# Scores from one product over 192 keys in two runs, in an attention and MoE kernel whose order is drawn by a planner

## The chip, the core and the metric

One core of a Trainium2 chip runs the kernel. The metric is the device time of one execution in microseconds (us). The profile is of one execution. The engines are TensorE (PE; its weight loads are PEld), VectorE (DVE), ScalarE (ACT), GpSimd (POOL) and SyncE (SP), which issues the DMAs.

## What is computed

An attention with a local window and a few global keys, and behind it a gated mixing layer (the code calls it MoE). Batch 4, 8 heads of 64 dimensions, 768 positions.

```python
scores = scale * np.matmul(q, k.transpose(0, 1, 3, 2))
is_global = pos[None, :] < int(n_global)          # 8
is_local = (rel >= 0) & (rel < int(n_local))      # 96
dist = np.where(is_global & ~is_local, float(n_local), np.abs(rel).astype(np.float32))
scores = scores + (-slopes[:, None, None] * dist[None, :, :])[None]
scores = np.where(is_global | is_local, scores, -1000000000.0)
a = np.exp(scores - np.max(scores, axis=-1, keepdims=True))
a = a / (np.sum(a, axis=-1, keepdims=True) + 1e-09)
x = np.matmul(a, v)                               # then heads side by side: 512 columns
...
h = gelu(x @ w_in); u, v = halves of h
v_s = np.einsum('ts,bsd->btd', w_sg, layernorm(v) * g_ln) + b_sg
out = x + (u * v_s) @ w_out
```

## The kernel before

*Attention units.* The attention is cut into 48 units `n`: a batch, a pair of heads `j`, and a third `u` of the sequence, which holds two tiles `i` of 128 queries. A half of a tile is 64 queries (`e`, `HQ`). Since the window is at most 97 wide (`NL_FAST`) and at most 32 first keys are global (`NG`), 64 queries need 192 keys (`W`): 96 near ones which both halves of the tile share, 64 others of the half's own, and the 32 first keys of the sequence. The first tile of a sequence (`u == 0 and i == 0`) needs just its own 128 keys.

*Tiles.* `load_qk` (L773) brings one tile `qk` per unit: 256 columns of queries, then up to 448 of keys (`KW`), laid out on the host by `unit_keys`. Three such tiles exist. `load_v` brings `v` in the key order that the p.v products want. The array of TensorE is used in quarters of 64x64: `h` (the head) picks the rows, `e` the output partitions, so four products run side by side. MoE products use the whole array.

*A unit's steps.* `score` (L786) fills two PSUM banks `s_ps`, one a head. `softmax` (L813) adds the bias row and takes the minimum of the negated scores on VectorE (L825), does exp with its sum on ScalarE (L830), then the reciprocal (L843). The first 16 units (`TURNS`) turn the probabilities with products against a diagonal (`turn_quarters`, `tps`, L929) and copy them to `pt` on ScalarE or VectorE (L937, L938). The later units scale them on GpSimd or another engine (L851), transpose blocks on VectorE (`tt`, L893) and send them through DRAM and back (`far`, L901 and L905) into `pt`. `weigh` (L941) then multiplies with `v`: a first part, and a second part `again` that follows after a score group has gone between. From unit 20 on two units go together.

*Bias.* `dist` is made once, at the start, on VectorE (L734 to L745) from tiles that GpSimd's iota fills; `build_bias` (L763) multiplies it by a head's slope into `bias[:, h]`. The two heads of a pair keep their 192 keys in two orders (the 96 shared keys and the 32 first ones in the first 128 columns for one head, in the last 128 for the other), so that a row is 2 x 192 + 128 = 512 wide. The last 128 are for the first tile of a sequence.

*MoE.* Each output tile is a row of products in threes (L466 to L468: high by high, high by low, low by high), 128x384 or 128x512. `v_tile`, `u_tile`, `mix_tile` and `out_tile` give these; their results go through ScalarE and VectorE.

*The order.* Nothing is issued in the order in which it is written. `Plan` collects operations with prices by engine, draws 40 sets of rules and shifts from a fixed seed (`search`, L253), orders the work by each (`order`, L278), and keeps the one that ends first by its own prices. It knows that going from whole-array to quarter products and back costs time (`TO_QUARTERS`, `FROM_QUARTERS`, L103), prices a score group at 0.56 or 0.67 (L811), a load by its width (`wire`, L770), and holds `dist` back to a fixed time (`dist_b.since`, L753). Within the first 29 us `keep_on` (L404) fills expected idle time of TensorE with products of zeros (L415). The instructions of each engine then run in the order found. So any changed price or time can move work on every engine.

Of the kernel before, what the change touches and what calls it, by code (L numbers as in the profile page):

```python
# [19 lines left out]
P = 128  # L20
# [8 lines left out]
NG = 32  # L29
# [7 lines left out]
W = P + HQ  # L37
KW = 3 * P + HQ
VT = 2 * P
# [34 lines left out]
def unit_widths(u):  # L74

    return (P + NG + P + NG, P + VT) if u == 0 else (KW, 2 * VT)


def unit_keys(u):

    t, first = 2 * u * P, list(range(NG))
    if u == 0:
        return list(range(P)) + first + list(range(P - NG, 2 * P))
    return (list(range(t - 3 * NG, t - NG)) + first + list(range(t - NG, t + P)) + first
            + list(range(t + P - NG, t + 2 * P)))
# [563 lines left out]
def local_global_attention_moe(tc, qk_in, v_in, q_t, k_t, v_n, n_gl, w_in, g_ln, w_sg_t, b_sg,  # L649
# [43 lines left out]

    bias = cp.tile([P, H, 2 * W + P], BF16, name="bias")

# [4 lines left out]
    rel, key, tmp = (zp.tile([P, W + P], BF16, tag=f"gt{i}", name="setup") for i in (1, 2, 3))  # L700
    dist = zp.tile([P, 2 * W + P], BF16, tag="gt0", name="dist")
    for p0, shared, other in ((0, NG, 3 * NG), (HQ, 3 * NG, 0)):
        ps = slice(p0, p0 + HQ)
        iota(rel[ps, 0:NG], S, 0, 0)
        iota(rel[ps, NG:P], shared, -1, 1)
        iota(rel[ps, P:W], other, -1, 1)
    iota(key[:, 0:NG], 0, 1, 0)
    iota(key[:, NG:W], S, 0, 0)
    iota(rel[:, W:W + P], 0, -1, 1)
# [23 lines left out]
    def distances():  # L733
# [7 lines left out]
        vec.scalar_tensor_tensor(tmp, rel, nl, key, ALU.is_ge, ALU.mult)  # L741
        vec.scalar_tensor_tensor(dist[:, 0:W], rel[:, 0:W], nl, tmp[:, 0:W], ALU.min, ALU.max)
        vec.scalar_tensor_tensor(dist[:, 2 * W:], rel[:, W:], nl, tmp[:, W:], ALU.min, ALU.max)
        for src, dst, n in ((0, HQ, P), (P, 0, HQ)):
            vec.tensor_copy(dist[:, W + dst:W + dst + n], dist[:, src:src + n])  # L745

# [16 lines left out]
    def build_bias(j):  # L763
        for h in (2 * j, 2 * j + 1):
            op([("DVE_SB", 0.22, 0.3, lambda h=h: nc.vector.tensor_scalar(
                bias[:, h], dist, -(2.0 ** (2 - h)), None, ALU.mult)),
                on_act(2 * W + P) + (lambda h=h: nc.scalar.mul(
                    bias[:, h], dist, -(2.0 ** (2 - h))),)], [dist_b], [(bias_b, h)])
# [17 lines left out]
    def score(n, after):  # L786

        b, j, u = units[n]
        qk = loaded.pop(n)
        s_ps = scores[n] = [bank("s_ps", 2 * W) for _ in range(2)]  # L790

        def part(h, e, i, k0, c0, n):
            rows, qc = slice(h * D, (h + 1) * D), i * P + e * HQ
            nc.tensor.matmul(s_ps[h][e * HQ:(e + 1) * HQ, i * W + c0:i * W + c0 + n],  # L794
                             qk[rows, qc:qc + HQ], qk[rows, QW + k0:QW + k0 + n],
                             start=True, stop=True)

        def put():
            quarters = [(h, e) for h in range(2) for e in range(2)]
            for i in range(2):  # L800
                if u == 0 and i == 0:
                    for h, e in quarters:
                        part(h, e, i, 0, 0, P)
                    continue

                for h, e in quarters:
                    part(h, e, i, window(u, i, e)[0], 0 if h == i else HQ, P)
                for h, e in quarters:
# [69 lines left out]
    def turn_blocks(n):  # L878
# [20 lines left out]
        def there():  # L899
# [8 lines left out]

        order = [0, 1, 2, 4, 3] if own else [0, 2, 1, 3, 5, 4]
        turned[n] = to, lambda rows, a, q0, q1: to[  # L910
            rows, q0 // QB:q1 // QB, order[a] * QB:(order[a] + 1) * QB]

    def turn_quarters(n):

        own, ps, diag = units[n][2] == 0, soft.pop(n), diags.pop(n)
        at = [(0, c) for c in ((0, W) if own else (0, 2 * P, P))] + [
            (1, c) for c in (0, 2 * P, P)]
        nt = len(at)
# [22 lines left out]
    def weigh(ns):  # L941
# [21 lines left out]
        def shared(m, second):  # L963
            for r, h in quarters:
                i = (r + h + second) % 2

                part(m, i, r, h, v0[i] + h * D, a0[i] + (i + h) % 2, 0, P,
                     start=not second and m == 0)

        def put():  # L970
            for m in range(len(ns)):
                shared(m, 0)
                for e in range(2):
                    for r, h in quarters:
                        i = (r + h) % 2
                        if u or i:
                            part(m, i, r, h, v0[i] + P + e * D, a0[i] + 2, e * HQ, (e + 1) * HQ,
                                 start=False)
# [417 lines left out]
```

## Time and profile before

| what | value |
|---|---|
| timed runs | 420.73, 421.56, 422.47 us; median 421.56 |
| span of the profiled execution | 420.1 us (the page gives no other time for it) |
| mean granted clock of TensorE | 0.993 |
| bytes read and written in HBM | 48.89 MB and 18.35 MB, 160 GB/s over the span |
| TensorE instructions | 5224 products and as many weight loads |

A row of the groups has line, engine, operation, output<-input tiles, shape and count, then busy time and the mean of one in ns, then the engine's idle time just before such instructions and what ended it. A row of the timeline has start, duration, engine, line, operation, tiles, shape and count. Durations of TensorE's products overlap, so the distance from start to start tells what one costs. The first 85 us hold most of the attention of the first batch, before MoE work is there in plenty; from about 100 us TensorE has MoE products to put between attention steps, and the last 75 us are MoE alone.

### The profile page before, as it was taken

How to read it: one execution, taken by the hardware profiler on the slowest of the kernel's cores; microseconds unless marked ns; L12 is line 12 of the kernel's file. 1: busy time of each engine (PE TensorE's matmuls, PEld its weight loads, DVE VectorE, ACT ScalarE, POOL GpSimd, SP SyncE). 2: the span in 40 equal slices, each digit the busy share in tenths (PEclk: the TensorE clock that was granted, in tenths of full speed). 3: DMA queues.
4: the chain of work that ended last, by engine and by line, in shares of the span. 5: the costliest groups of instructions: out<-in, count | busy, mean ns of one | idle time of the engine just before them, and what ended most of it. 6: DMA issues, size and time to landing. Idle time of an engine off the chain costs nothing.

```text
span 420.1 us, 13632 instructions
## 1 busy us (share of the span) xinstructions
PE 403.7 (96%) x5224; PEld 368.2 (88%) x5224; DVE 323.5 (77%) x1037; ACT 228.2 (54%) x744; POOL 174.6 (42%) x306
## 2 busy tenths in 40 slices
PE   8888989999999999999999999999999999999994
PEld 5766867899998889799999989999999888999994
DVE  6787989999997699995777899885768578754362
ACT  5898889765765765753356556653255343311220
POOL 2234447365686646353554355442553122303100
PEclk9999999989999999999999999999999999999998
DMA  7666575526877778754798785562886521001002
GB/s 246 201 208 166 154 238 153 158 81 173 240 249 255 192 228 238 208 162 114 211 271 227 226 240 141 155 170 54 244 281 172 152 85 39 2 2 48 29 0 81
DMA packets 50040, 68.20 MB, mean 162 GB/s; under 512 B 5809, under 2 KB 33969, under 8 KB 49969
## 3 DMA queue, kind: packets, MB, share of 16 engines
q1 hardware_dynamic: 49968, 67.26, 54.7%
q8 instruction: 43, 0.70, 0.8%
q14 instruction: 29, 0.23, 0.2%
HBM read 48.89 MB, written 18.35 MB: 160 GB/s over the span
## 4 chain that ended last, share of the span: by engine, by line
PE 79%; ACT 6%; DVE 5%; DMA 4%; issue 3%; POOL 1%; SPq 1%; DVEq 0%; POOLq 0%; ACTq 0%
PE mm_ps L466 22%; PE mm_ps L467 21%; PE mm_ps L468 21%; PE s_ps L794 6%; PE av L959 6%; PE tps L929 2%; ACT p L830 2%; DMA pt<-far 2%; DMA qk<-in_qk_in_dram 1%; DMA far<-tt 1%; DVE p L825 1%; DMA v<-in_v_in_dram 1%; ACT stage L631 1%; ACT wsg L641 1%; ACT pt L937 0%
## 5 line engine op out<-in xcount | busy, mean ns | idle before, releaser
L830 ACT ACTIVATE p<-p,pst 128x192 f32<-128x192 f32 (+1 forms) x192 | 84.0, 440 | 36.8 <-DVE pst L825 34.9
L466 PE MATMUL mm_ps<-wsg,z 128*128 128x384 f32 x192 | 65.5, 341 | 0.1
L467 PE MATMUL mm_ps<-wsg,z 128*128 128x384 f32 x192 | 64.9, 338 | 0.0
L468 PE MATMUL mm_ps<-wsg,z 128*128 128x384 f32 x192 | 64.8, 338 | 0.0
L825 DVE CUSTOM_DVE_ANT_0 p<-s_ps,bias 128x192 f32<-128x192 f32 (+1 forms) x192 | 56.5, 337 | 5.1 <-PE s_ps L794 4.9
L851 POOL TENSOR_SCALAR p<-p,pst 128x192 f32<-128x192 f32 (+1 forms) x111 | 50.4, 470 | 15.0 <-DVE pst L843 14.8
L959 PE MATMUL av<-pt,v 64*64 64x128 f32 (+1 forms) x1408 | 47.6, 250 | 1.2 <-DMA pt<-far 1.2
L592 POOL TENSOR_TENSOR o<-o,x 128x384 f32<-128x384 f32 x28 | 28.4, 1013 | 47.5 <-DVE o L589 25.8
L794 PE MATMUL s_ps<-qk 64*64 64x128 f32 (+1 forms) x1408 | 43.1, 249 | 4.1 <-issue 2.5
L794 PEld LDWEIGHTS s_ps<-qk 64*64 64x64 f32 x1408 | 37.1, 134 | 8.9 <-issue 5.7
L466 PE MATMUL mm_ps<-x,win 128*128 128x384 f32 x128 | 44.0, 343 | 0.7 <-ACT pt L937 0.7
L959 PEld LDWEIGHTS av<-pt,v 64*64 64x64 f32 x1408 | 37.2, 134 | 8.2 <-issue 4.9
L468 PE MATMUL mm_ps<-gt,wout 128*128 128x384 f32 x128 | 43.1, 336 | 0.1
L466 PE MATMUL mm_ps<-gt,wout 128*128 128x384 f32 x128 | 43.1, 337 | 0.0
L467 PE MATMUL mm_ps<-gt,wout 128*128 128x384 f32 x128 | 42.9, 335 | 0.0
L468 PE MATMUL mm_ps<-x,win 128*128 128x384 f32 x128 | 42.9, 335 | 0.0
L467 PE MATMUL mm_ps<-x,win 128*128 128x384 f32 x128 | 42.9, 335 | 0.0
L466 PE MATMUL mm_ps<-win,x 128*128 128x512 f32 x96 | 39.6, 412 | 0.0
L500 ACT CAST gt<-y 128x384 fp32r<-128x384 f32 x27 | 13.8, 511 | 46.2 <-DVE y L561 33.4
L467 PE MATMUL mm_ps<-win,x 128*128 128x512 f32 x96 | 37.7, 393 | 0.0
L468 PE MATMUL mm_ps<-win,x 128*128 128x512 f32 x96 | 37.6, 392 | 0.0
L466 PEld LDWEIGHTS mm_ps<-wsg,z 128*128 128x128 f32 x192 | 36.5, 190 | 1.1 <-issue 0.5
(109 smaller groups left out, 905.2 us busy)
## 6 DMA issues: line engine op xcount, KB each, us to landing
qk<-in_qk_in_dram SPq DMA_DIRECT2D x32, 352.0 KB, 3.9
far<-tt SPq DMA_DIRECT2D x96, 96.0 KB, 2.6
pt<-far SPq DMA_DIRECT2D x24, 384.0 KB, 3.9
v<-in_v_in_dram SPq DMA_DIRECT2D x32, 256.0 KB, 3.7
out_dram<-o SPq DMA_DIRECT2D x32, 192.0 KB, 2.7
qk<-in_qk_in_dram SPq DMA_DIRECT2D x16, 288.0 KB, 3.8
v<-in_v_in_dram SPq DMA_DIRECT2D x16, 192.0 KB, 3.6
far<-tt SPq DMA_DIRECT2D x32, 80.0 KB, 2.2
```

The source lines that it names most:

```text
L466: mm(ps.ap, ah, bh, start=(i == 0), stop=False)
L467: mm(ps.ap, ah, bl, start=False, stop=False)
L468: mm(ps.ap, al, bh, start=False, stop=(i == n - 1))
L500: put(out[:, 0, :], src.ap)
L592: lo = lambda eng: eng.tensor_tensor(o.ap, o.ap, xm[:, 1, :].bitcast(F32), ALU.add)
L631: op([on_act(n, 0.07) + (lambda: nc.scalar.mul(f.ap, words()[:, :, 1].bitcast(F32), 2.0 ** -112),)], [raw], [f])
L794: nc.tensor.matmul(s_ps[h][e * HQ:(e + 1) * HQ, i * W + c0:i * W + c0 + n], qk[rows, qc:qc + HQ], qk[rows, QW + k0:QW + k0 + n], start=Tru ...
L825: nc.vector.tensor_tensor_reduce(out=p[:, g, 0:nk], in0=s_ps[h][:, i * W:i * W + nk], in1=bias[:, 2 * j + h, w0:w0 + nk], op0=ALU.add, op1 ...
L830: op([on_act(nk, 0.225) + (lambda p=p, g=g, nk=nk, i=i: nc.scalar.activation(p[:, g, 0:nk], p[:, g, 0:nk], AF.Exp, bias=st[:, 0, i, g:g + ...
L851: op([on_pool_ts(nk, -0.10) + (partial(scaled, lambda o, a, c: nc.gpsimd.tensor_scalar(o, a, c, 1.0, ALU.mult, ALU.mult)),), on_act(nk, 0. ...
L929: nc.tensor.matmul(tps[r][g * HQ:(g + 1) * HQ, a * HQ:(a + 1) * HQ], pc[rows, c:c + HQ], diag[rows, 2 * i + c // W], start=True, stop=True)
L959: nc.tensor.matmul(to, v[rows, vc:vc + D], of, stop=True, skip_group_check=True, **kw)
```

## The change

The host lays the 192 keys of each half-tile out as two runs of 96: `near` (the 96 shared keys), and `before` or `after` (the 32 first keys and the half's own 64). A tile's three runs stand one behind the other, six runs a unit, so that `KW` becomes 576 and `qk` 832 columns wide, keys first and queries behind them. The first keys stand there twice for each tile. A score product then reads both runs with one access pattern (`p (b k)`, step 96 or 192) and writes 192 columns at once; before, it took a product over 128 keys and one over 64. Both heads have the same key order now: the bias row is 192 + 128 = 320 wide, `dist` needs no second copy, `turn_blocks`, `turn_quarters` and `weigh` pick their columns by other indices, and the host swaps the halves of `v` rows for one head. The price of a score in the plan stays; that of a bias row and `dist_b.since` (6.35 to 6.0) fall.

```diff
-KW = 3 * P + HQ
+NS = P - NG
+KW = 6 * NS
...
+def tile_keys(t):
+    first = list(range(NG))
+    return (list(range(t - NG, t + HQ)), first + list(range(t - 3 * NG, t - NG)),
+            first + list(range(t + HQ, t + P)))
...
 def window(u, i, e):
     if u == 0:
-        return P, (NG, 2 * P)[e]
-    return ((HQ, (0, HQ + P)[e]) if i == 0 else (2 * P, (HQ + 3 * NG, 3 * P)[e]))
+        return 0, (NS, NS + P)[e]
+    return 3 * NS * i, 3 * NS * i + NS * (1 + e)
...
-    bias = cp.tile([P, H, 2 * W + P], BF16, name="bias")
+    bias = cp.tile([P, H, W + P], BF16, name="bias")
...
-        vec.scalar_tensor_tensor(dist[:, 0:W], rel[:, 0:W], nl, tmp[:, 0:W], ALU.min, ALU.max)
-        vec.scalar_tensor_tensor(dist[:, 2 * W:], rel[:, W:], nl, tmp[:, W:], ALU.min, ALU.max)
-        for src, dst, n in ((0, HQ, P), (P, 0, HQ)):
-            vec.tensor_copy(dist[:, W + dst:W + dst + n], dist[:, src:src + n])
+        vec.scalar_tensor_tensor(dist, rel, nl, tmp, ALU.min, ALU.max)
...
-    dist_b.since = 6.35
+    dist_b.since = 6.0
...
-            op([("DVE_SB", 0.22, 0.3, lambda h=h: nc.vector.tensor_scalar(
+            op([("DVE_SB", 0.17, 0.25, lambda h=h: nc.vector.tensor_scalar(
                 bias[:, h], dist, -(2.0 ** (2 - h)), None, ALU.mult)),
-                on_act(2 * W + P) + (lambda h=h: nc.scalar.mul(
+                on_act(W + P) + (lambda h=h: nc.scalar.mul(
...
-        def part(h, e, i, k0, c0, n):
-            rows, qc = slice(h * D, (h + 1) * D), i * P + e * HQ
-            nc.tensor.matmul(s_ps[h][e * HQ:(e + 1) * HQ, i * W + c0:i * W + c0 + n],
-                             qk[rows, qc:qc + HQ], qk[rows, QW + k0:QW + k0 + n],
-                             start=True, stop=True)
+        q0 = unit_widths(u)[0]
+        def part(h, e, i):
+            rows, qc = slice(h * D, (h + 1) * D), q0 + i * P + e * HQ
+            to, n = s_ps[h][e * HQ:(e + 1) * HQ], W
+            if u == 0 and i == 0:
+                keys, n = qk[rows, NS:NS + P], P
+            else:
+                near, far = window(u, i, e)
+                step = far - near
+                keys = qk[rows, near:near + 2 * step].rearrange("p (b k) -> p b k", k=step)[:, :, 0:NS]
+                to = to[:, i * W:(i + 1) * W].rearrange("p (b k) -> p b k", k=NS)
+            if n == P:
+                to = to[:, i * W:i * W + n]
+            nc.tensor.matmul(to, qk[rows, qc:qc + HQ], keys, start=True, stop=True)
...
-                for h, e in quarters:
-                    part(h, e, i, window(u, i, e)[0], 0 if h == i else HQ, P)
-                for h, e in quarters:
-                    part(h, e, i, window(u, i, e)[1], P if h == i else 0, HQ)
+                for h in range(2):
+                    for e in range(2):
+                        part(h, e, i)
...
-                w0, nk = (2 * W, P) if own else (g * W, W)
+                w0, nk = (W, P) if own else (0, W)
...
-        order = [0, 1, 2, 4, 3] if own else [0, 2, 1, 3, 5, 4]
         turned[n] = to, lambda rows, a, q0, q1: to[
-            rows, q0 // QB:q1 // QB, order[a] * QB:(order[a] + 1) * QB]
+            rows, q0 // QB:q1 // QB, a * QB:(a + 1) * QB]
...
-                part(m, i, r, h, v0[i] + h * D, a0[i] + (i + h) % 2, 0, P,
+                g = (h - i) % 2
+                a = g if u == 0 and i == 0 else (0, 2 - r)[g]
+                part(m, i, r, h, v0[i] + h * D, a0[i] + a, 0, P,
                      start=not second and m == 0)
```

The order of TensorE's instructions moves with it; lines of the changed kernel are 8 further down (L466 is L474, L794 is L812, L959 is L967). In the rows that follow `s_ps<-qk` is a score product, `av<-pt,v` a p.v product, `tps<-diag,p` a transpose by product, and `mm_ps` a MoE product. The first place is after some 210 us of before, in the steady part; before it stood, on TensorE:

```order
L467 MATMUL mm_ps<-gt,wout 128x384
L468 MATMUL mm_ps<-gt,wout 128x384
L794 MATMUL s_ps<-qk 64x128 x4
L794 MATMUL s_ps<-qk 64x64 x4
L794 MATMUL s_ps<-qk 64x128 x4
L794 MATMUL s_ps<-qk 64x64 x4
L959 MATMUL av<-pt,v 64x128 x4
L959 MATMUL av<-pt,v 64x64 x8
```

In the changed program the same place on TensorE reads:

```order
L476 MATMUL mm_ps<-gt,wout 128x384
L812 MATMUL s_ps<-qk 64x192 x8
L474 MATMUL mm_ps<-x,win 128x384
L475 MATMUL mm_ps<-x,win 128x384
L476 MATMUL mm_ps<-x,win 128x384
L967 MATMUL av<-pt,v 64x128 x4
L967 MATMUL av<-pt,v 64x64 x8
```

Sixteen score products became eight, and three MoE products moved in between the score group and the p.v products.

The second place is the one at about 82 us of before, where unit 15 is turned; TensorE's rows there in before:

```order
L468 MATMUL mm_ps<-wsg,z 128x384
L959 MATMUL av<-pt,v 64x128 x4
L959 MATMUL av<-pt,v 64x64 x4
L929 MATMUL tps<-diag,p 64x64 x20
L794 MATMUL s_ps<-qk 64x128 x4
L794 MATMUL s_ps<-qk 64x64 x4
```

And in the changed program, on TensorE, from the same transposes on:

```order
L967 MATMUL av<-pt,v 64x64 x4
L937 MATMUL tps<-diag,p 64x64 x20
L474 MATMUL mm_ps<-x,win 128x384
L475 MATMUL mm_ps<-x,win 128x384
L476 MATMUL mm_ps<-x,win 128x384
```

Nine more MoE products follow before the score group: twelve now stand where the score group followed at once.

More of the change, by code (lines that the diff above doesn't have):

```diff
@@ L74, in unit_widths @@
 def unit_widths(u):
-    return (P + NG + P + NG, P + VT) if u == 0 else (KW, 2 * VT)
+    return (2 * NS + P, P + VT) if u == 0 else (KW, 2 * VT)
+def tile_keys(t):
+    first = list(range(NG))
+    return (list(range(t - NG, t + HQ)), first + list(range(t - 3 * NG, t - NG)),
+            first + list(range(t + HQ, t + P)))
 def unit_keys(u):
-    t, first = 2 * u * P, list(range(NG))
+    t = 2 * u * P
     if u == 0:
-        return list(range(P)) + first + list(range(P - NG, 2 * P))
-    return (list(range(t - 3 * NG, t - NG)) + first + list(range(t - NG, t + P)) + first
-            + list(range(t + P - NG, t + 2 * P)))
+        near, _, after = tile_keys(P)
+        return near + list(range(P)) + after
+    return sum((keys for i in range(2) for keys in tile_keys(t + i * P)), [])
 def window(u, i, e):
     if u == 0:
-        return P, (NG, 2 * P)[e]
-    return ((HQ, (0, HQ + P)[e]) if i == 0 else (2 * P, (HQ + 3 * NG, 3 * P)[e]))
+        return 0, (NS, NS + P)[e]
+    return 3 * NS * i, 3 * NS * i + NS * (1 + e)
 SYNC = 0.07
@@ L976, in put @@
                         if u or i:
[L977 removed]
+                            part(m, i, r, h, v0[i] + P + e * D, a0[i] + 1 + r, e * HQ, (e + 1) * HQ,
                                  start=False)
@@ L1363 @@
                 continue
-            shared = first + list(range(i * P - NG, i * P + HQ))
-            other = list(range(i * P - 3 * NG, i * P - NG)), list(range(i * P + HQ, (i + 1) * P))
-            v_in[:, :, u, :, v0:v0 + P] = vp[:, :, shared]
+            near, before, after = tile_keys(i * P)
+            shared, other = near + list(range(NG)), (before[NG:], after[NG:])
+            for g in range(2):
+                hd = slice((i + g) % 2 * D, ((i + g) % 2 + 1) * D)
+                rows = shared[HQ * g:] + shared[:HQ * g]
+                v_in[:, :, u, :, v0 + hd.start:v0 + hd.stop] = vp[:, :, rows, hd]
             for e in range(2):
```

25 lines of the change are left out of this document (10 added, 15 removed).

## The prediction

> **What bounds the kernel now.** I read the page first (busy shares, then the chain that ended last), then the busy time by stretches of time, then TensorE's own waits, and last its instructions in order of time at the places that matter.
>
> ```profile
> span 420.1 us, 13632 instructions
> PE 403.7 (96%) x5224; PEld 368.2 (88%) x5224; DVE 323.5 (77%) x1037; ACT 228.2 (54%) x744; POOL 174.6 (42%) x306
> ...
> PE 79%; ACT 6%; DVE 5%; DMA 4%; issue 3%; POOL 1%; SPq 1%; DVEq 0%; POOLq 0%; ACTq 0%
> ...
> L794 PE MATMUL s_ps<-qk 64*64 64x128 f32 (+1 forms) x1408 | 43.1, 249 | 4.1 <-issue 2.5
> ```
>
> TensorE works through 96% of the span and is 79% of the chain. So the reader should ask of every edit how long TensorE is occupied by it, and treat the other engines as causes of TensorE's waits. The score products are the last row: 1408 instructions, which is two passes for each of the program's 704 products.
>
> ```profile
> 70.00:80.00 10.00, 9.30 (x138) 8.81 (x137) 9.64 (x25) 10.00 (x34) 4.93 (x8) 1.00 0.52 151
> 80.00:90.00 10.00, 8.35 (x121) 7.61 (x120) 9.79 (x34) 6.42 (x23) 3.45 (x5) 0.83 0.20 68
> ...
> 200.00:340.00 140.00, 140.00 (x1689) 131.63 (x1692) 107.63 (x353) 68.36 (x231) 61.62 (x115) 1.00 0.69 196
> ```
>
> The columns are stretch, length, busy time of PE, PEld, DVE, ACT and POOL, then the granted clock, the DMA share and GB/s. From 200 to 340 us TensorE has no idle time at all: there any added TensorE work lengthens the kernel in full, and any saved work shortens it in full. From 70 to 90 us the stage is another one: TensorE is idle for 0.70 and 1.65 us, while VectorE (9.64, 9.79) and, in its first half, ScalarE (10.00) are full; and the granted clock falls to 0.83.
>
> ```profile
> PE s_ps L794 <- issue: 2.5, 2, 1.3
> PE tps L929 <- issue: 2.0, 3, 0.9
> PE s_ps L794 <- ACT pt L937: 1.5, 1, 1.5
> ...
> PE av L959 <- DMA pt<-far: 1.2, 2, 0.8
> ...
> PE mm_ps L466 <- ACT pt L937: 0.7, 1, 0.7
> ```
>
> These are TensorE's own waits (total, times, longest). They are few and small, and a changed order can remove or add them.
>
> **The change, part by part.** Term 1, *one product for two*. The chain shows what groups of scores take when they follow other small products:
>
> ```profile
> 211.60 0.67 PE s_ps L794 x32
> ...
> 236.34 0.55 PE s_ps L794 x24
> ```
>
> A group of 32 is a unit with two full tiles: four products run side by side on the four quarters of the array, so it is four rounds over 128 keys and four over 64. A group of 24 (the first unit of a sequence) is four rounds over 128 and two over 64. With 0.11 us for 128 keys and 0.0575 us for 64 both come out (4 x 0.11 + 4 x 0.0575 = 0.67; 4 x 0.11 + 2 x 0.0575 = 0.555). Then 64 keys more cost 0.0525 us, and a round costs about 0.005 us apart from its keys. The keys streamed stay the same, 192 a row; only rounds go: four in each of 32 units, two in each of 16, 160 rounds, 160 x 0.005 = 0.8 us. The rows are rounded to 0.01, so the fixed part could be anything from 0 to about 0.0125 (then 0.06 and 0.1075 fit): **0 to 2.0 us saved, I take 0.8.** The 133 ns weight loads that go lie beside running products and buy nothing more.
>
> The moving operand is now two runs of 96 keys with a gap. The trace of before has no such read in a score, but it has a more broken one:
>
> ```profile
> L959 PE MATMUL av<-pt,v 64*64 64x128 f32 x304 | 14.1, 273 | 0.0
> ...
> L794 PE MATMUL s_ps<-qk 64*64 64x128 f32 x256 | 12.1, 277 | 0.0
> ```
>
> These rows are of 200 to 340 us alone, where `pt` is read as four runs of 32 (the tile of `turn_blocks`), and a pass takes 273 ns against 277 for the unbroken keys. So I take nothing for the gap. The Trainium skill (Advanced Engine Details and Errata, section Memory Cachelines) says of PSUM that any non-contiguous access pattern slows matmuls significantly. It gives no price; these two rows speak against it for runs of this length on the moving side.
>
> Term 2, *the planner deals the work out anew*. The planner's price for a score is unchanged, but wider `qk` loads, cheaper bias rows and an earlier `dist` change its draws. The order on TensorE shows what came of it: the stretches of quarter products (scores, transposes, p.v) that have MoE products ahead of them number 35 before and 44 after. What it costs to go into such a stretch and out again is read where one score group stands alone:
>
> ```profile
> 187.93 0.34 PE L468 MATMUL mm_ps<-x,win 128*128 128x384 f32 x1
> 188.19 0.90 PE L794 MATMUL s_ps<-qk 64*64 64x128 f32 x32
> 189.02 0.44 PE L466 MATMUL mm_ps<-x,win 128*128 128x384 f32 x1
> 189.31 0.34 PE L467 MATMUL mm_ps<-x,win 128*128 128x384 f32 x1
> 189.48 0.34 PE L468 MATMUL mm_ps<-x,win 128*128 128x384 f32 x1
> ```
>
> From the start at 187.93 to that at 189.31 pass 1.38 us. In it lie two 384-wide products at their usual distance of 0.17 (189.31 to 189.48) and the group's 0.67: 1.02 in all. **One way in and out costs 0.36 us.** Of the nine more, five lie beyond 200 us (in before's times at 213, 225, 263, 305 and 318), where a score group is now cut off by three or six MoE products from the p.v products that followed it at once. The 200:340 row has no idle time that the cut could fill, so they cost 5 x 0.36 = +1.8. One more lies between 100 and 200 us, where TensorE waits little: +0.4. Three lie between 70 and 90 us: +1.1, against what they fill (term 3). Together **+3.3 us**; the bounds are 0 (each fills a wait of its own length) and 3.3.
>
> Term 3, *what the cuts near 70 to 90 us fill*. Here is the wait in before:
>
> ```profile
> 82.70 0.40 PE L794 MATMUL s_ps<-qk 64*64 64x128 f32 x3
> 84.63 0.77 PE L794 MATMUL s_ps<-qk 64*64 64x128 f32 x24 [1.53 <-ACT pt L937]
> ...
> 86.50 0.47 PE L466 MATMUL mm_ps<-wsg,z 128*128 128x384 f32 x1
> 86.77 0.52 PE L467 MATMUL mm_ps<-wsg,z 128*128 128x384 f32 x1
> 87.09 0.52 PE L468 MATMUL mm_ps<-wsg,z 128*128 128x384 f32 x1
> ...
> 89.65 0.49 PE L467 MATMUL mm_ps<-wsg,z 128*128 128x384 f32 x1
> 89.97 0.34 PE L468 MATMUL mm_ps<-wsg,z 128*128 128x384 f32 x1
> ```
>
> The second bank of that score group is freed only by a ScalarE copy of `pt`, so TensorE stands for 1.53 us, and two microseconds later its products come every 0.32 us in place of 0.17, for 3.4 us: the half clock that the 80:90 row shows as 0.83 (10 us x 0.17 = 1.7 us lost). In the changed order twelve MoE products (12 x 0.17 = 2.1 us) stand between the transposes and this score group, more than the wait. If TensorE is busy there, the wait goes, and with it probably the spell at half clock: -1.5 and -1.7. The other wait of that stage (0.7, ahead of a 384-wide product) lies where ScalarE is busy 10.00 of 10 us; products put ahead of it only reach ScalarE's queue sooner, so I take nothing for it. **Sum -3.2, bounds 0 and -3.9.** What is late next is VectorE, busy 9.79 of 10 us; the 9.41 of 90 to 100 us behind it does not hold up TensorE.
>
> Is the half clock due to that wait? The row says that it followed, and that waits of up to 1.3 us earlier (the first row of TensorE's waits) were not followed by one. The Trainium skill (TensorE: Matmul & The Clock Gate, section Part 1: The HAM clock gate) asks for a whole idle window of about 3.4 us before the clock halves, which 1.53 us is not. By that rule alone the spell would have another cause and stay, and the sum below would end at 422.9.
>
> Term 4, *wider keys*. Each of 32 loads moves 64 KB more (the tile grows from 704 to 832 columns):
>
> ```profile
> qk<-in_qk_in_dram SPq DMA_DIRECT2D x32, 352.0 KB, 3.9
> ...
> 100.00:110.00 10.00, 10.00 (x119) 9.33 (x121) 9.26 (x29) 7.10 (x23) 4.79 (x7) 1.00 0.93 254
> ```
>
> At 254 GB/s, with the queues 0.93 busy, 64 KB take 0.26 us. Three `qk` tiles are loaded ahead, so it lies under other work except where TensorE waits for a transfer anyway: bounds 0 and 32 x 0.26 = 8.3; I take one such place, +0.3. SyncE issues no more DMAs than before.
>
> Term 5, *bias*. The last step of `dist` loses two copies, and the bias rows shrink from 512 to 320:
>
> ```profile
> 5.87 0.28 DVE L745 COPY dist<-dist 128x128 bf16<-128x128 bf16 x2
> 6.18 0.29 DVE L765 TENSOR_SCALAR bias<-dist 128x512 bf16<-128x512 bf16 x1
> 6.62 0.29 DVE L825 CUSTOM_DVE_ANT_0 p<-s_ps,bias 128x128 f32<-128x128 f32 x1 [0.15 <-PE s_ps L794]
> ```
>
> The first softmax waits 0.15 us for TensorE, not for the bias. The 0.3 us won ahead of it is hidden by the first scores; eight bias rows at about 0.1 us less come to 0.8 us on VectorE and ScalarE, spread over the first 10 us. I take 0; bounds -0.8 and 0.
>
> The other edits cost nothing of themselves: the tile order in `turn_blocks`, `turn_quarters` and `weigh` changes which columns are read, not how many products, copies or DMAs there are. The planner also puts more filler products of `keep_on` where it expects an idle TensorE in the first 29 us: 97 now, 72 before.
>
> ```profile
> L415 PEld LDWEIGHTS <-bsg 128*128 128x128 bf16 x72 | 6.7, 105 | 5.2 <-issue 2.0 <-DVE bsg L676 1.2
> ```
>
> If TensorE were not idle there, 25 more would cost at most 25 x 0.105 = 2.6 us; since TensorE's longest waits (1.3 us) lie in that part, I take 0 and keep the bound.
>
> **Sum:** -0.8 + 3.3 - 3.2 + 0.3 = -0.4 us on the profiled span of 420.1. The page gives no other time for that execution; the timed runs lie 0.6 to 2.4 us above the span (420.73 to 422.47), and the -0.4 is set against their median: 421.56 - 0.4 = **421.2 us**.
>
> **The rivals.** *Slower: the cuts are not repaid.* One mechanism, the ways in and out of quarter products on a TensorE without idle time. All of +3.3 is paid, with +0.3 and -0.8, and the wait at 84 us and its half clock come back elsewhere: 421.56 + 2.8 = 424.4. For it speaks that VectorE, not TensorE, is full at 70 to 90 us; against it that twelve products are more than the wait needs. It decides when less than 0.7 of the 3.2 us is won (2.8 - 0.7 = 2.1, the 0.5%). Chance 0.19.
>
> *Faster: the new order also fills the early waits.* Add to the forecast the 0.7, both waits for `pt<-far` (1.2) and half of the 4.5 us that TensorE stood in the first 60 us for no shown reason: -0.4 - 0.7 - 1.2 - 2.25 = -4.6, 417.0. For it speaks that all instructions around these waits were dealt out anew; against it that the same deal may open others. Chance 0.26.
>
> *The product does not do what it says.* If a read of two runs ran at half pace, 160 rounds of 0.16 us would double: +25.6 - 0.4, 446.8. The 273 and 277 ns speak against it. Chance 0.02.
>
> The forecast, no change that can be seen, has 0.53. About 0.5% (2.1 us) is what a measurement of this kernel can tell from no change. The range reaches to the rivals on both sides, 417.0 to 424.6, since together they hold nearly half. Faster 0.26, same 0.53, slower 0.21 (the last two rivals).
>
> **What would show it.** Score groups of 16 instructions in about 0.65 us (0.67 now) show term 1; a group of 0.8 or more refutes it. A way in and out of 0.36 us in the five cuts after 200 us, with TensorE still idle for nothing there, shows term 2. A granted clock of 1.00 in every stretch from 70 to 100 us, and no wait of a score group for a `pt` copy there, shows term 3. The prediction is wrong if new waits of more than 2 us stand on TensorE, if a second spell at half clock appears, or if a score waits for its `qk` load.

## The result, and the profile after

| | before | changed |
|---|---|---|
| median of the timed runs, same chip | 421.14 us (418.63 to 422.47) | 427.11 us (426.74 to 427.33) |
| ratio, with its 95% interval | | 1.0138 (1.0097 to 1.0179) |
| span of the profiled execution | 420.1 us | 425.0 us |

The change makes the kernel slower by 1.4%. The forecast was 421.2 with a range up to 424.6; the measured time lies outside that range. The half clock is not what sets the two apart: the four timed runs of the changed kernel lie within 0.6 us of each other at mean granted clocks from 0.992 to 0.998, and the profiled execution has 0.995, 0.993 before.

From the page of the changed kernel, the lines that answer to those of before:

```profile
span 425.0 us, 12394 instructions
PE 406.8 (96%) x4609; PEld 363.0 (85%) x4609; DVE 315.7 (74%) x1030; ACT 223.3 (53%) x729; POOL 190.4 (45%) x326
...
PE 67%; DVE 11%; DMA 10%; ACT 4%; SPq 3%; issue 3%; POOL 1%; DVEq 0%; POOLq 0%; ACTq 0%
...
L812 PE MATMUL s_ps<-qk 64*64 64x192 f32 (+1 forms) x768 | 41.3, 320 | 1.1 <-DMA qk<-in_qk_in_dram 0.5
```

The product does what it says: 768 instructions in place of 1408. But TensorE's share of the chain falls from 79% to 67%, while transfers rise from 4% to 10% and VectorE from 5% to 11%: something other than TensorE's own work now sets the end in places. The busy sum cannot tell how much, since it counts the fillers (97, 72 before) and the overlap of neighbouring products at each way in and out.

The busy times by stretches show where (columns as before: stretch, length, PE, PEld, DVE, ACT, POOL, granted clock, DMA share, GB/s):

```profile
70.00:80.00 10.00, 9.95 (x110) 9.10 (x109) 9.68 (x29) 8.38 (x25) 6.78 (x9) 1.00 0.66 205
80.00:90.00 10.00, 9.58 (x121) 8.49 (x120) 9.49 (x28) 7.12 (x22) 6.20 (x10) 1.00 0.32 102
90.00:100.00 10.00, 10.00 (x90) 9.58 (x89) 9.93 (x27) 7.57 (x23) 8.18 (x11) 1.00 0.37 99
100.00:110.00 10.00, 7.99 (x81) 7.24 (x83) 7.64 (x24) 4.40 (x16) 4.18 (x8) 1.00 0.78 249
110.00:120.00 10.00, 9.78 (x97) 9.06 (x93) 9.41 (x32) 7.36 (x24) 7.96 (x12) 1.00 0.66 215
120.00:130.00 10.00, 8.77 (x88) 7.33 (x84) 5.28 (x17) 4.29 (x16) 3.89 (x9) 1.00 0.98 297
```

From 70 to 100 us the stage is as forecast: TensorE works, and the clock is 1.00. From 100 to 110 us TensorE had no idle time before (10.00); now it stands for 2.01 us. From 120 to 130 us it stands for 1.23 us, while the DMA engines are 0.98 busy. TensorE's waits (total, times, longest):

```profile
PE av L967 <- DMA pt<-far: 3.5, 3, 1.6
PE mm_ps L476 <- DVE win L651: 1.3, 1, 1.3
...
PE mm_ps L474 <- ACT wsg L649: 0.9, 1, 0.9
```

The waits for `pt` copies are gone. In their place p.v waits 3.5 us for `pt<-far` (1.2 before), and MoE products wait for the splitting of weights that have just been loaded (`win`, `wsg`). Here is the longest, on TensorE and then in the chain of the same kernel (start, length):

```profile
106.85 0.34 PE L476 MATMUL mm_ps<-gt,wout 128*128 128x384 f32 x1
108.82 0.68 PE L967 MATMUL av<-pt,v 64*64 64x128 f32 x24 [1.64 <-DMA pt<-far]
```

```profile
102.69 5.99 DMA pt<-far
...
113.06 4.50 DMA stage<-in_w_sg_t_dram
...
169.41 4.72 DMA pt<-far
```

One transfer of 384 KB is under way for 5.99 us. What stands around it on SyncE (start, time to issue, line, tiles), after and then before:

```profile
97.75 3.30 SPq L910 DMA_DIRECT2D far<-tt  x4
101.16 0.38 SPq L790 DMA_DIRECT2D v<-in_v_in_dram  x1
101.58 0.45 SPq L783 DMA_DIRECT2D qk<-in_qk_in_dram  x1
102.12 0.38 SPq L636 DMA_DIRECT2D stage<-in_w_out_dram  x1
102.69 0.33 SPq L914 DMA_DIRECT2D pt<-far  x1
103.11 0.38 SPq L636 DMA_DIRECT2D stage<-in_w_out_dram  x1
103.55 1.21 SPq L632 DMA_DIRECT2D stage<-in_w_sg_t_dram  x2
```

```profile
98.60 1.78 SPq L901 DMA_DIRECT2D far<-tt  x4
100.43 0.45 SPq L777 DMA_DIRECT2D qk<-in_qk_in_dram  x1
100.97 0.38 SPq L784 DMA_DIRECT2D v<-in_v_in_dram  x1
101.90 0.33 SPq L905 DMA_DIRECT2D pt<-far  x1
103.90 1.42 SPq L628 DMA_DIRECT2D stage<-in_w_out_dram  x3
```

In both programs a unit's turned probabilities go out to `far`, and loads are issued while SyncE would otherwise wait for them to land. Before, two loads stood there, and the next DMA followed 2.0 us after `pt<-far`. Now there are three loads ahead, one of them 64 KB larger, and three weight loads close behind. Before, this transfer landed after 4.5 us and no product waited for it. A long landing alone is not the loss: before has one of 6.2 us too, issued at 130.76, and nothing waits for it there. It costs time where the order leaves TensorE nothing to do meanwhile.

To add up the small waits as well, I give each product of the trace its usual distance to the next (0.17 us for 384 columns, 0.23 for 512, and for a quarter product a fourth of 0.057, 0.11 or 0.163 us for 64, 128 or 192 columns; fillers get none). With these rounded distances every entry of the table comes out 1.2 to 1.9 us higher; the differences between the rows of a column stay the same to 0.2 us. What is left of a stretch is TensorE's **loss** there: waits, ways in and out, half clock.

| loss of TensorE, us | 0 to 100 | 100 to 200 | 200 to 340 | span |
|---|---|---|---|---|
| before | 31.0 | 7.4 | 4.4 | 420.1 |
| changed | 27.3 | 12.0 | 7.2 | 425.0 |

The changed kernel wins 3.7 us by 100 us and gives back 4.6 in the next hundred, and 2.8 after that. Another 1.4 us lie behind the last product (from its start to the end of the span 7.15 us, 5.69 before); e7 below has 5.7 there, e8 7.1, and e1, in the old order, 7.3, so I put it down neither to the change nor to the order.

### The profile page after: what moved, and what is told of

The parts are those of the page before. It is cut to its first block, busy times and chain, and to the rows that moved or that the text cites. A ratio compares the mean times of both kernels' runs of the same rounds, so it can differ in the third digit from the quotient of the medians.

```text
span 425.0 us, 12394 instructions
## 1 busy us (share of the span) xinstructions
PE 406.8 (96%) x4609; PEld 363.0 (85%) x4609; DVE 315.7 (74%) x1030; ACT 223.3 (53%) x729; POOL 190.4 (45%) x326
## 4 chain that ended last, share of the span: by engine, by line
PE 67%; DVE 11%; DMA 10%; ACT 4%; SPq 3%; issue 3%; POOL 1%; DVEq 0%; POOLq 0%; ACTq 0%
PE mm_ps L474 18%; PE mm_ps L476 17%; PE mm_ps L475 17%; PE av L967 6%; PE s_ps L812 6%; DMA pt<-far 4%; DMA far<-tt 3%; DMA qk<-in_qk_in_dram 2%; ACT p L839 2%; SPq L910 2%; PE tps L937 2%; DVE tt L902 1%; DMA stage<-in_w_sg_t_dram 1%; DVE p L834 1%; DVE stage L646 1%
## 5 line engine op out<-in xcount | busy, mean ns | idle before, releaser
L474 PE MATMUL mm_ps<-wsg,z 128*128 128x384 f32 x192 | 65.1, 339 | 0.9 <-ACT wsg L649 0.9
L860 POOL TENSOR_SCALAR p<-p,pst 128x192 f32<-128x192 f32 (+1 forms) x122 | 54.8, 466 | 8.2 <-DVE pst L852 7.8
L967 PEld LDWEIGHTS av<-pt,v 64*64 64x64 f32 x1408 | 40.0, 133 | 13.4 <-issue 8.3
L967 PE MATMUL av<-pt,v 64*64 64x128 f32 (+1 forms) x1408 | 47.8, 251 | 3.8 <-DMA pt<-far 3.5
L474 PE MATMUL mm_ps<-x,win 128*128 128x384 f32 x128 | 44.4, 347 | 0.1
L474 PE MATMUL mm_ps<-gt,wout 128*128 128x384 f32 x128 | 43.2, 338 | 0.0
L812 PE MATMUL s_ps<-qk 64*64 64x192 f32 (+1 forms) x768 | 41.3, 320 | 1.1 <-DMA qk<-in_qk_in_dram 0.5
L508 ACT CAST gt<-y 128x384 fp32r<-128x384 f32 x29 | 14.8, 511 | 49.9 <-DVE y L569 27.9
L474 PE MATMUL mm_ps<-win,x 128*128 128x512 f32 x96 | 39.8, 415 | 0.0
L474 PEld LDWEIGHTS mm_ps<-wsg,z 128*128 128x128 f32 x192 | 36.0, 188 | 2.9 <-ACT wsg L649 1.4
L902 DVE STREAM_TRANSPOSE tt<-p 128x384 f32<-128x384 f32 (+1 forms) x64 | 32.6, 540 | 7.0 <-DMA far<-tt 5.7
```

The lines of the kernel that those rows point to most:

```text
L474: mm(ps.ap, ah, bh, start=(i == 0), stop=False)
L508: put(out[:, 0, :], src.ap)
L812: nc.tensor.matmul(to, qk[rows, qc:qc + HQ], keys, start=True, stop=True)
L860: op([on_pool_ts(nk, -0.10) + (partial(scaled, lambda o, a, c: nc.gpsimd.tensor_scalar(o, a, c, 1.0, ALU.mult, ALU.mult)),), on_act(nk, 0. ...
L902: nc.vector.transpose(out, src.rearrange("p g (b j) -> p g b j", j=QB))
L967: nc.tensor.matmul(to, v[rows, vc:vc + D], of, stop=True, skip_group_check=True, **kw)
```

## The experiments

The first question: is it the new code or the order that the planner drew from its new prices? All runs, with the kernel before on the same chip in the same session:

| run | median, us | kernel before, us | ratio (95%) |
|---|---|---|---|
| e1 new code, old order | 419.49 | 422.61 | 0.995 (0.9918 to 0.9982) |
| e2 old code, new order | 428.26 | 422.61 | 1.0123 (1.007 to 1.0175) |
| e3 narrow loads, new order | 424.55 | 422.61 | 1.0047 (1.0018 to 1.0075) |
| e4 narrow loads, old order | 419.2 | 422.61 | 0.994 (0.9912 to 0.9968) |
| e5 `pt<-far` first, new order | 452.41 | 420.83 | 1.0708 (1.0613 to 1.0803) |
| e6 `pt<-far` first, old order | 445.68 | 420.83 | 1.0581 (1.0511 to 1.065) |
| e7 new prices, second start | 423.56 | 420.83 | 1.0064 (1.0037 to 1.0091) |
| e8 new prices, third start | 421.12 | 420.83 | 1.0003 (0.9969 to 1.0037) |
| e9 old prices, second start | 422.31 | 420.69 | 1.0033 (1.0002 to 1.0065) |
| e10 old prices, third start | 423.02 | 420.69 | 1.004 (1.001 to 1.0069) |
| e11 light loads, new order | 420.49 | 420.69 | 0.9994 (0.9966 to 1.0022) |
| e12 light loads, old order | 419.52 | 420.69 | 0.997 (0.9947 to 0.9994) |
| e13 transfers at 280 GB/s | 418.17 | 419.94 | 0.9954 (0.9928 to 0.9981) |
| e14 the same, second start | 421.77 | 419.94 | 1.0048 (1.0017 to 1.0079) |
| e15 the same, third start | 418.64 | 419.94 | 0.9972 (0.9954 to 0.9991) |

The kernel before moves by up to 2.7 us from session to session, so I compare ratios, and turn them into microseconds at 421.

**e1: the new code in the old order.** The changed kernel with the four prices of before, which gives the old order on every engine:

```diff
-    dist_b.since = 6.0
+    dist_b.since = 6.35
...
-            op([("DVE_SB", 0.17, 0.25, ...
+            op([("DVE_SB", 0.22, 0.3, ...
-                on_act(W + P) + ...
+                on_act(2 * W + P) + ...
...
-        op([wire(kw) + ...
+        op([wire(QW + (2 * P + 2 * NG if u == 0 else 3 * P + HQ)) + ...
```

> The changed kernel with the four prices of before in its planner (load width, bias rows, dist_b.since), so that every engine has before's order of instructions; 192-key products, 832-column loads and 320-wide bias stay. Theory A (the order that the planner drew is the whole loss): 420.5 us, that is before's 421.1 less 0.7 for the score groups; groups of 16 instructions in 0.65 us, the half clock near 86 us is back. Rival B (64 KB more per load make the DMA round trips late): 425 us or more, with waits of TensorE for pt<-far. Rival C (the two-run read or the new code itself is slow somewhere): also 425 us or more, without such waits.

**e2: the old code in the new order.** The kernel before with the same four places the other way round.

> The kernel before with the four prices of the change in its planner, so that every engine has the changed kernel's order; two products, 704-column loads and 512-wide bias stay. Theory A: 427.8 us, the changed kernel's 427.1 plus 0.7 for the longer score groups, with the waits for pt<-far near 107 and 173 us. Rival B: about 422, since the loads are narrow. Rival C: 421 to 422.

**e3 and e4: narrow loads.** The new code with loads of `qk` as wide as before (704 columns), in the new order and in the old:

```diff
-        op([wire(kw) + (lambda: nc.sync.dma_start(qk[:, 0:kw], qk_in[b, j, u][:, 0:kw]),)],
+        op([wire(kw) + (lambda: nc.sync.dma_start(qk[:, 0:kw - P * (u > 0)], qk_in[b, j, u][:, 0:kw - P * (u > 0)]),)],
...
-        q0 = unit_widths(u)[0]
+        q0 = unit_widths(u)[0] - P * (u > 0)
```

> The changed kernel, order unchanged, but the last 128 columns of each wide qk tile are not loaded (704 columns; the queries are read 128 columns further ahead, so the scores are of other data). Theory A: 427, no change by more than 1 us. Rival B: 423 or less, and the waits for pt<-far near 107 and 173 us shrink to under 0.5 us each. Rival C: 427.

> The changed kernel with before's order (as the run with the old prices), and the last 128 columns of each wide qk tile not loaded, so the scores are of other data. Theory A: the same as with the wide loads, 420.5 within 1 us. Rival B: 420 here and 425 with the wide loads. Rival C: 425.

Theory A fits e1, e2 and e4. e3 lies between the theories (427, or 423 and less), and p.v still waits 2.6 us for `pt<-far` in it.

The order is the main part. In the new code it costs 1.0138 - 0.995 = 0.019, 7.9 us; in the old code 0.012, 5.2 us. The new code by itself saves: in the old order it is 0.5% faster than the kernel before, and faster than both kernels. The width costs what its order lets it: 0.001 (0.4 us, inside the intervals) in the old order, 0.009 (3.8 us) in the new. The 5.8 us (0.0138) of the change thus add up from three steps: the new code with narrow loads in the old order -2.5 (e4), the new order with the same loads +4.5 (e3 less e4), the wider loads in that order +3.8. Each step is known to about 2 us either way.

**e5 and e6: `pt<-far` ahead of the loads.** If loads in front of `pt<-far` are what delays it, they can go behind it. The list that the planner hands out is altered on SyncE alone:

```diff
-        for o in self.search(start):
+        for o in far_first(self.search(start)):
...
+def far_first(done):
+    done = list(done)
+    for o in [o for o in done if o.dma and any(b.kind == "far" for b in o.bufs)
+              and any(b.kind == "pt" for b in o.bufs)]:
...
+        for x in late:
+            done.remove(x)
+        k = done.index(o)
+        done[k + 1:k + 1] = late
+    return done
```

> The changed kernel with one thing altered: where a load of q and k, of v or of a weight stands on SyncE between the four `far<-tt` transfers of a unit and its `pt<-far`, it is issued right behind the `pt<-far` (all loads but nothing else; TensorE's order is that of the changed kernel). Theory C, the loss between 100 and 200 us is the way of the turned probabilities behind loads: the waits of the p.v products for `pt<-far` (3.5 us in three places) fall below 1 us, the `pt<-far` at 102 us lands about 3 us after its issue in place of 6, and the time is 427.1 - 3 = about 424. Theory D, TensorE is only ahead of the whole transfer stream there (weights too), and what one transfer gains another loses: the pt wait falls but the waits for the weights' staging (0.9 and 1.3 us) or for `qk` and `v` grow by as much, 426 to 428.

> The new code with the old prices and so the old order on every engine but SyncE, where loads go behind `pt<-far` as in e5. Theory C: the old order waits 0.7 us for `pt<-far` and 1.4 us for loads of `v`; the first goes, 418.5 to 419.5. Theory D: the waits only change places, 419.5 to 421. A rise above 422 would say that loads of `qk` or `v` cannot stand being three microseconds later.

Both theories missed the size: 452 and 446. TensorE's waits and SyncE in e5:

```profile
PE av L967 <- DMA v<-in_v_in_dram: 5.9, 4, 2.9
PE s_ps L812 <- DMA qk<-in_qk_in_dram: 4.7, 5, 2.1
PE mm_ps L474 <- ACT wsg L649: 3.5, 1, 3.5
PE s_ps L812 <- DVE tt L902: 2.4, 1, 2.4
```

```profile
97.54 1.81 SPq L910 DMA_DIRECT2D far<-tt  x4
102.27 0.34 SPq L914 DMA_DIRECT2D pt<-far  x1
102.66 0.42 SPq L790 DMA_DIRECT2D v<-in_v_in_dram  x1
103.14 0.42 SPq L783 DMA_DIRECT2D qk<-in_qk_in_dram  x1
```

The wait for `pt<-far` is gone as theory C said, but loads of `v`, `qk` and weights are late everywhere. SyncE stands from 99.35 to 102.27 us with nothing to issue, since `pt<-far` waits for `far` to land, and everything behind it waits too. So the loads between the two are well placed. Whether it is their bytes that hurt, e11 below asks. Theory D has the direction, but it allowed for 1 us, and the step costs 24 (1.0708 against 1.0138). Part of that is half clock, which the longer waits brought with them: the mean granted clock of the profiled execution is 0.983 (0.995 in the changed kernel), some 5 us of its 449.

**e7 to e10: other draws.** One number, in the changed kernel (e7, e8) and in e1 (e9, e10):

```diff
-        rnd = random.Random(1)
+        rnd = random.Random(2)
```

(3 in e8 and e10.)

> The changed kernel with another start of the planner's random numbers (2 in place of 1), all prices new: 36 stretches of quarter products in place of 44. Theory A1, the loss is an unlucky draw: 418 to 423, like e1 or a little above. Theory A2, the new prices themselves make worse orders (for instance since the wider loads now hold the planner's wire longer): 425 or more, like the changed kernel.

> As e7 with a third start (3): 36 stretches of quarter products. Theory A1: 418 to 423; theory A2: 425 or more. The two draws together also show how far apart two orders of the same work lie; by A1 they differ from each other by some microseconds and both lie below the changed kernel.

> The new code with the four old prices (as e1) and the second start of the random numbers; 37 stretches of quarter products. Theory A1, a draw is worth some microseconds and the new prices nothing: 420 to 426, about what the new prices gave with the same start (423.6). Theory A2, the new prices make worse orders: 418 to 420.5, like e1, below 423.6 by 3 or more.

> As e9 with the third start; 39 stretches of quarter products. Theory A1: 420 to 426, so that e1 (419.5) was a good draw among the old prices; theory A2: 418 to 420.5, below the 421.1 of the new prices with this start.

Three draws of the new prices give ratios of 1.0138, 1.0064 and 1.0003, three of the old 0.995, 1.0033 and 1.004. The changed kernel is the worst of the six and e1 the best; theory A1 holds for the most part (e7 lies 0.6 us above its 423). The first start is a bad one for the new prices and a good one for the old. Whether the new prices are worse on the whole cannot be told from three draws each.

**e11 and e12: light loads.** What makes the bad order bad? Both orders, with half of the loads' bytes in the later units:

```diff
-        ... nc.sync.dma_start(qk[:, 0:kw], qk_in[b, j, u][:, 0:kw]),)],
+        ... nc.sync.dma_start(qk[:, 0:kw if u == 0 else 2 * NS + QW], qk_in[b, j, u][:, 0:kw if u == 0 else 2 * NS + QW]),)],
...
-        ... nc.sync.dma_start(v[:, 0:vw], v_in[b, j, u][:, 0:vw]),)], [], [v])
+        ... nc.sync.dma_start(v[:, 0:vw if u == 0 else VT], v_in[b, j, u][:, 0:vw if u == 0 else VT]),)], [], [v])
...
-                near, far = window(u, i, e)
+                near, far = window(u, i, e) if u == 0 else (0, 2 * NS)
```

(with `q0` at `2 * NS` and both tiles' `v` in the same columns for the later units)

> The changed kernel in its own order, with about half of what the later units load: of q and k 224 KB in place of 416, of v 128 in place of 256 (the products read the same columns twice, so scores and outputs are not those of the reference; counts and sizes of products, copies and of the transfers of turned probabilities stay). Theory T, what the new order loses against the old it loses to transfers: the waits for `pt<-far` (3.5 us) and for the weights' staging (2.2) mostly go, and the time is within 1.5 us of e12, 419 to 420.5. Theory O, it loses by its order on the engines (cuts, dependencies): 4 us or more above e12, 422.5 to 424.5.

> The control to e11: the new code in the old order (e1) with the same halved loads. e1 without its wait of 1.4 us for a load of v, and nothing else: 418 to 419. If this falls to 416 or lower, the loads cost the old order more than its waits show, and e11 is to be read against it.

These two answer it. With light loads the new order costs 0.0024 (1.0 us, inside the intervals) more than the old, where it cost 7.9. Halving the bytes is worth 1.0138 - 0.9994 = 0.0144, 6.1 us, in the new order, and nothing in the old one (0.995 and 0.997). The two lie 1.0 us apart, as theory T said, and TensorE has 81% of e11's chain, transfers 3%. TensorE's waits in e11 no longer have a `pt<-far` among them; the longest is one that the changed kernel has too:

```profile
PE mm_ps L476 <- DVE win L651: 1.6, 1, 1.6
PE s_ps L423 <- DVE bsg L684: 1.2, 1, 1.2
PE tps L423 <- issue: 0.8, 1, 0.8
```

By stretches, in the measure of the table above:

| loss of TensorE, us | 0 to 100 | 100 to 200 | 200 to 340 | span |
|---|---|---|---|---|
| changed | 27.3 | 12.0 | 7.2 | 425.0 |
| e1, old order | 29.1 | 7.1 | 5.6 | 419.6 |
| e3, narrow, new order | 26.6 | 10.8 | 7.0 | 422.8 |
| e11, light, new order | 27.4 | 7.3 | 6.8 | 419.1 |
| e12, light, old order | 27.3 | 7.3 | 4.8 | 417.1 |
| e13, transfers at 280 GB/s | 29.9 | 7.0 | 4.8 | 418.9 |

What the new order loses between 100 and 200 us goes altogether with the loads' bytes (12.0 to 7.3, where the old order has 7.1 and 7.3). After 200 us light loads change little: the new order keeps 6.8 against 4.8.

**e13 to e15: dearer transfers.** The planner reckons loads and `pt<-far` at 360 GB/s; the 120:130 row shows 297 with the engines 0.98 busy. (Stretches of 10 us in other runs show more than the 297 of the expectation: 306 in e3, 316 in e10.) The three places at 280, with the three starts:

```diff
-        return "SP", 0.38, P * words * 4 / 360e3
+        return "SP", 0.38, P * words * 4 / 280e3
```

> The changed kernel with its new prices, but the planner reckons each load and each `pt<-far` at 280 GB/s in place of 360 (the traces show at most 297 GB/s with the DMA engines 0.98 busy); first start of the random numbers, 38 stretches of quarter products. Theory P, the orders of the new prices lose between 100 and 200 us because the planner takes transfers for cheaper than they are: TensorE loses 7 to 8 us between 100 and 200 us (12.0 in the changed kernel), and the time is 417 to 421. Theory A1, it is the draw alone: the loss there and the time lie anywhere between those of the six draws so far, 419.5 to 427, with p.v still waiting 1 us or more for `pt<-far`.

> As e13 with the second start; 41 stretches of quarter products. Theory P: 7 to 8 us lost between 100 and 200 us (8.7 with the price of 360 GB/s), 417 to 421; theory A1: anything from 419.5 to 427.

> As e13 with the third start; 41 stretches of quarter products. Theory P: 7 to 8 us lost between 100 and 200 us (10.7 with the price of 360 GB/s), 417 to 421; theory A1: anything from 419.5 to 427. By theory P the three also lie within 2 us of each other, where the three draws of the new prices at 360 GB/s lie 6 apart (427.1, 423.6, 421.1).

Start for start the ratios are 0.9954, 1.0048 and 0.9972 in place of 1.0138, 1.0064 and 1.0003. The first and the third do what theory P said (7.0 and 7.3 us lost between 100 and 200 us, though the execution profiled of the third, 422.6 us, is one of its longest; medians 418.2 and 418.6). The second misses by 0.8 us: it loses 9.5 us there, and p.v still waits once, for 1.7 us, on `pt<-far`. The three lie 3.6 us apart, not within 2. Only with the first start is the gain clear of the intervals (0.9928 to 0.9981 against 1.0097 to 1.0179), and that start was the worst of six draws, so that another order could hardly have come out slower. That the price is part of the cause is therefore suggested, by the fall of the loss in two of three draws, and not shown; luck remains. e13 is one of the versions that beat both kernels, as e1 and e15 are; their intervals overlap. Its stretch from 100 to 130 us, where the changed kernel's TensorE is busy for 26.55 us:

```profile
100.00:130.00 30.00, 29.76 (x316) 27.64 (x308) 26.46 (x85) 19.73 (x68) 20.84 (x32) 1.00 0.84 259
```

## Why the prediction was wrong, step by step

*Term 1, one product for two (-0.8): the mechanism right, the size at the low end.* The chain has groups of 16 where it had groups of 32, at 0.65 us for 0.67:

```profile
213.05 0.65 PE s_ps L812 x16
```

e1 shows the new code alone at 0.2 to 0.8% below the kernel before, which is 0.8 to 3.5 us, and e4, without the wider loads, at 1.3 to 3.7 us. Where the rest beyond the 0.02 us a group comes from, no run separates.

The Trainium skill (Advanced Engine Details and Errata, section Memory Cachelines) says that non-contiguous access patterns in PSUM slow matmuls. Here the PSUM side is unbroken and only the moving keys are two runs with a gap, where no such thing shows: the 192 columns with the gap take less than 128 and 64 without one.

*Term 2, the cuts (+3.3): the price and the late ones right.* Where a group stands alone after 200 us:

```profile
210.12 0.34 PE L476 MATMUL mm_ps<-gt,wout 128*128 128x384 f32 x1
210.39 0.88 PE L812 MATMUL s_ps<-qk 64*64 64x192 f32 x16
211.20 0.44 PE L474 MATMUL mm_ps<-x,win 128*128 128x384 f32 x1
211.48 0.33 PE L475 MATMUL mm_ps<-x,win 128*128 128x384 f32 x1
```

From 210.12 to 211.48 pass 1.36 us; less two distances of 0.17 and 0.65 for the group, a way in and out is 0.37 (forecast 0.36). Five such cuts were to cost 1.8 beyond 200 us. e11 has five more stretches of quarter products there than e12, and with the loads light it loses 2.0 more.

*Term 3, what the early cuts fill (-3.2): the mechanism seen, the size not shown to be its own.* The wait at 84 us is gone and the clock is 1.00 from 70 to 100 us, with 3.7 us less lost by 100 us. But e1 has the old order, and the old wait, without the half clock:

```profile
83.73 0.70 PE L812 MATMUL s_ps<-qk 64*64 64x192 f32 x10 [1.44 <-ACT pt L945]
...
84.96 0.44 PE L474 MATMUL mm_ps<-wsg,z 128*128 128x384 f32 x1
85.23 0.34 PE L475 MATMUL mm_ps<-wsg,z 128*128 128x384 f32 x1
85.41 0.35 PE L476 MATMUL mm_ps<-wsg,z 128*128 128x384 f32 x1
```

So the 1.7 us belong to that execution and not to the order. Without them the changed kernel wins 2.0 us by 100 us, against before, and 1.8 against e1 (27.3 and 29.1). The light loads say the same, though the table has 27.4 and 27.3 there: e11 happens to hold a half clock of 3.4 us, 1.7 lost, in its first 100 us (mean granted clock 0.98, shown at the end), and e12 has none (1.00). Without it the new order wins 1.6. Terms 2 and 3 forecast -1.5 + 1.1 = -0.4 for that stage without the half clock, so the new order filled more there than the one wait; with what, no run tells.

*Term 4, wider keys (+0.3), and what the sum left out: the step that failed.* "It lies under other work except where TensorE waits for a transfer anyway ... I take one such place": the widening costs 3.8 us in the new order (the changed kernel against e3), and that order's exposure to the loads comes to 6.1 (against e11). The widening is not all of it: with the old width the new order still costs 4.5 us (e3 less e4; terms 2 and 3 came to +0.1), and with light loads 1.0. So about as much again as the widening, some 3.5 us, is a cost with no term in the sum: the new order moves the transfers as well as TensorE's products. I counted SyncE's issues and not their places. The trace of before had the row that warned: 0.93 busy from 100 to 110 us, and TensorE without idle time, so that nothing there covered later transfers. The planner's new order put more loads around `pt<-far`, and TensorE came to wait for it. "What is late next is VectorE" was wrong too; it was the transfers. The order of SyncE stood open before the run; it shows the loads around `pt<-far`, though not what they would cost. Two of the signs that the prediction named for its being wrong came: 3.5 us of new waits, and scores that wait for their `qk` loads, 0.5 us in two places.

With it goes the clause of term 2 that "one more lies between 100 and 200 us, where TensorE waits little": I carried the waits of before into an order that has others.

*Term 5 and the fillers (0):* nothing in the stretches speaks against it; neither was tried alone.

*The rivals and the range.* The slower rival gave 424.4 by cuts that are not repaid; the kernel is slower, but by transfers. I wrote a bound of 8.3 us for term 4 and then let the range end at 424.6. With 3 us of it in the range, 427.1 would have been inside.

## What to carry to other kernels

Where an order is drawn anew, compare the DMA queue's order first: what stands between a transfer and the one that depends on it, and how busy the DMA engines are there. A price in a planner is an input to a lottery: here a change of four prices moved the time by up to 1.9% with the same code, and three starts of the same prices lay up to 1.35% apart, more than the edit is worth, so the new code is to be judged in the old order (e1) as well. Setting a transfer's price nearer to the rate that full stretches show made a better order with one start, clear of the intervals, and with the other two no change that is.

## What the runs showed of the hardware

The half clock is not bound to the wait ahead of it. Here is one in e11, right behind a wait of 1.61 us:

```profile
68.78 0.45 PE L476 MATMUL mm_ps<-x,win 128*128 128x384 f32 x1 [1.61 <-DVE win L651]
...
69.24 0.52 PE L475 MATMUL mm_ps<-x,win 128*128 128x384 f32 x1
69.56 0.52 PE L476 MATMUL mm_ps<-x,win 128*128 128x384 f32 x1
...
72.12 0.52 PE L475 MATMUL mm_ps<-x,win 128*128 128x384 f32 x1
72.44 0.43 PE L476 MATMUL mm_ps<-x,win 128*128 128x384 f32 x1
72.71 0.33 PE L474 MATMUL mm_ps<-x,win 128*128 128x384 f32 x1
```

From 69.24 to 72.44 us products come every 0.32 us. The same wait in the changed kernel (1.31 us) and the 1.44 us of e1 were followed by none. Nor does the length of the wait alone decide: e5 has one of 2.41 us with products at 0.23 us, their full pace, right behind it, and in e2 a half clock begins at 124 us where the waits just ahead were 1.06 and 0.79 us.

```profile
179.09 0.99 PE L812 MATMUL s_ps<-qk 64*64 64x192 f32 x16 [2.41 <-DVE tt L902]
...
180.35 0.39 PE L475 MATMUL mm_ps<-win,x 128*128 128x512 f32 x1
180.58 0.40 PE L476 MATMUL mm_ps<-win,x 128*128 128x512 f32 x1
```

The Trainium skill (TensorE: Matmul & The Clock Gate, section Part 1: The HAM clock gate) asks for an idle window of about 3.4 us, by which none of these waits would bring one. What decides between them stays open. Such spells go with the spread from run to run: of 91 timed runs of the kernel before, the 21 with a mean granted clock of 0.994 or less have a median of 422.1 us, and the 29 with 0.999 or more 420.1.

A transfer's time is no property of its size: `pt<-far` with its 384 KB took 5.99 us in the row at 102.69, while its median is 3.0 us in e5, where no load stands between `far<-tt` and it, and 4.3 in the changed kernel.
